# A gated mix of a long convolution and a feed-forward block: one two-stage 2048-point transform through DRAM in place of a four-block transform

## The chip, the cores and the metric

The kernel runs on one core of a Trainium2 chip. Its five engines each work through their own list of instructions: TensorE (PE in the profile, with its weight loads listed apart as PEld), VectorE (DVE), ScalarE (ACT), GpSimd (POOL) and SyncE (SP, which here only issues DMA transfers; SPq in a chain of waits is time spent issuing); 16 DMA engines move data between DRAM and on-chip memory. The time is device microseconds of one execution, median over several executions. A profile covers one execution and shows its span, which is 1.7 to 1.9 us less than the time of the same execution. "PE granted clock" is the share of full TensorE speed that the throttle allowed in a stretch.

## The reference, cut to what matters

There are 2048 tokens and 640 channels. Two things are computed from the same input and mixed with a gate:

```python
x = A_u                                                 # [1, 2048, 640] bf16
g = sigmoid((x * gate_w).sum(-1, keepdims=True))
# a: state-space convolution. For each channel d a kernel K[d, 0..2047] is built from 128 modes:
#    K[d, l] = Re sum_n C[d,n] * dt*B[d,n] * exp(dt*A[d,n] * l)
#    y = irfft(rfft(u, 4096) * rfft(K, 4096))[:2048] + u * Dskip
# b: feed-forward block, 640 -> 1728 -> 640
b = (gelu(x @ w_gate) * (x @ w_up)) @ w_down
return g * a + (1 - g) * b
```

The table K is the sum over 128 modes of complex exponentials. Both kernels split the position l into a coarse part and a fine part, so that exp(a·l) is a product of two short tables ("grid 1" and "grid 2", each with a cosine and a sine half), and the sum over modes is a contraction on TensorE, one small matrix product per channel.

## The kernel before

A helper class collects steps (engine, estimated time, buffers read and written) and orders them per engine with a list scheduler, so the program text isn't the order of execution. The convolution is done in four blocks of 512 tokens, each with a small transform. A product of spectra must therefore be formed for every pair of blocks, which is much work for VectorE:

```python
# parameters and tokens come in the layout of the model and are transposed by the DMA
def x_load(tq, kt):
    dma(1050, lambda: nc.sync.dma_start_transpose(out=xT[tq][:, kt, :], in_=u2[S*tq:S*tq+S, kt*128:kt*128+128]), ...)

# the contraction: one product of 128 weight columns x 84 per channel group and cos/sin half
for g in range(5):
    for q in range(2):
        nc.tensor.matmul(ps[:, k, 84*g:84*g+84], lhsT=cs1[c][:, q, k0+g, :], rhs=cs2[c][:, q, k0+g, :],
                         start=(q == 0), stop=(q == 1))

# spectral products, for block c from all blocks up to c (L904 is the one line tm that all use)
def tm(out, a, b, op):
    nc.vector.tensor_tensor(out=out, in0=a, in1=b, op=op)                     # L904
def mul(x, o, q):  ve(..., lambda: tm(x, u[:, ::1-2*q, rev, ds], kb[:, :, 0:n, ds], ALU.mult), ...)
def comb(x, o, q): ...                     # re*re - im*im and the like, also tm
def fold(x, o): ...
def last(x, o, q): ...
# ... cut: feed-forward gate (L588), up (L606), down (L994), spectra (L846, L866), inverse (L1015)
```

## Time and profile before

| | before |
|---|---|
| time, median of 3 runs | 351.43 us (350.82 to 351.55) |
| span of the profiled run | 355.9 us |
| PE / DVE / ACT busy | 299.7 / 297.8 / 237.2 us |
| moved by DMA | 25.5 MB |

The first fence is from the page of the kernel before: busy time of each engine with its share of the span, then three rows of the picture in 40 equal slices (each digit a busy share in tenths, PEclk the granted clock in tenths of full speed), the load of the DMA queue and the chain of work that ended last.

```profile
PE 299.7 (84%) x2182; PEld 175.8 (49%) x2182; DVE 297.8 (84%) x528; ACT 237.2 (67%) x374; POOL 15.7 (4%) x32
PE   0048459999999999999785679999999999999885
DVE  8999899756368898999893806999999999998962
PEclk9999988999999999999998989999999999999999
...
q1 hardware_dynamic: 52608, 23.79, 26.4%
...
DVE 38%; PE 27%; ACT 19%; SPq 10%; issue 4%; DMA 1%; another core or an unknown queue 0%; DVEq 0%; ACTq 0%
```

Two engines are at 84%, which reads as "nearly balanced", but the rows show that the limits lie in different stages: PE does next to nothing in the first two slices, and DVE is full from slice 26 on. The clock is full almost everywhere. The DMA is at 26%.

The second fence is from the groups of instructions of the kernel before (line, engine, operation, output and inputs, count, busy time and mean of one in ns, then the engine's idle time before them and what ended it).

```profile
L904 DVE TENSOR_TENSOR arena<-arena 128x640 bf16<-128x640 bf16 (+5 forms) x112 | 106.7, 1011 | 1.5 <-ACT arena L998 0.9
L588 PE MATMUL ps<-arena 128*128 128x512 bf16 x280 | 68.5, 396 | 25.9 <-DMA arena<-in_B_w_gate_dram 21.8
L994 PE MATMUL ps<-arena 128*128 128x320 bf16 x448 | 62.0, 299 | 0.4 <-ACT arena L872 0.4
```

The spectral products (L904) cost DVE 106.7 us. Of a matmul, the mean of one (396 ns) runs from its start to its modelled end, and neighbours overlap; busy time divided by count is what it costs: 68.5 / 280 = 0.245 us for 512 columns, and 62.0 / 448 = 0.138 us for 320.

The third is from the table of busy time by stretch of the kernel before (start:end, length, busy time of PE, PEld, DVE, ACT and POOL with instruction count, granted clock, DMA share, GB/s).

```profile
0.00:40.00 40.00, 12.71 (x35) 4.27 (x36) 37.79 (x107) 35.61 (x55) 6.10 (x22) 1.00 0.63 128
...
270.00:310.00 40.00, 40.00 (x315) 29.15 (x314) 39.93 (x42) 6.35 (x8) 0.00 (x0) 1.00 0.17 34
```

At the start PE is busy 12.71 of 40 us; near the end DVE is busy 39.93 of 40 us, and PE is full beside it.

### The profile page before, as it was taken

Reading aid. Unit: us, or ns where it says so; the run is one execution under the profiler, and the core shown is the slowest. Engines: PE = TensorE matmul, PEld = TensorE weight load, DVE = VectorE, ACT = ScalarE, POOL = GpSimd, SP = SyncE. Lnnn points to the kernel's source line nnn. Section 1 sums busy time; section 2 is a strip of 40 time slices with the busy share of each in tenths; the row PEclk is TensorE's granted clock in tenths of the full one; section 3 lists DMA queues with packets and bytes.
Section 4 is the critical chain, followed back from the end, with each engine's and each line's share of the span. In section 5 each row is a group of like instructions: output and inputs, shape, how many; then the busy total and the mean of one; then the engine's idle time right before and its main releaser. Section 6 shows DMA issues by size and latency. Waiting matters only on the chain.

```text
span 355.9 us, 5682 instructions
## 1 busy us (share of the span) xinstructions
PE 299.7 (84%) x2182; PEld 175.8 (49%) x2182; DVE 297.8 (84%) x528; ACT 237.2 (67%) x374; POOL 15.7 (4%) x32
## 2 busy tenths in 40 slices
PE   0048459999999999999785679999999999999885
PEld 0012113444555554444343545666777777767664
DVE  8999899756368898999893806999999999998962
ACT  6999699999999899999964779999111011100000
POOL 6000000000000000000071000000000000000000
PEclk9999988999999999999998989999999999999999
DMA  6684632003100201102552710052400005003321
GB/s 111 181 134 98 163 127 88 20 19 76 37 20 19 58 20 37 40 0 55 187 195 61 276 57 0 2 146 61 103 17 0 20 21 91 20 18 49 100 75 57
DMA packets 53019, 25.46 MB, mean 72 GB/s; under 512 B 46400, under 2 KB 50304, under 8 KB 52608
## 3 DMA queue, kind: packets, MB, share of 16 engines
q1 hardware_dynamic: 52608, 23.79, 26.4%
q0 software_dynamic: 384, 1.31, 1.2%
q8 instruction: 17, 0.28, 0.3%
q14 instruction: 10, 0.08, 0.1%
HBM read 12.83 MB, written 6.03 MB: 53 GB/s over the span
## 4 chain that ended last, share of the span: by engine, by line
DVE 38%; PE 27%; ACT 19%; SPq 10%; issue 4%; DMA 1%; another core or an unknown queue 0%; DVEq 0%; ACTq 0%
DVE arena L904 28%; PE ps L588 10%; PE ps L606 8%; SPq L302 7%; ACT arena L466 5%; ACT arena L529 3%; PE ps L524 3%; DVE arena L883 3%; ACT arena L592 3%; PE ps L1015 2%; ACT arena L430 2%; SPq L307 2%; DVE arena L1024 2%; PE ps L846 2%; ACT arena L660 2%
## 5 line engine op out<-in xcount | busy, mean ns | idle before, releaser
L904 DVE TENSOR_TENSOR arena<-arena 128x640 bf16<-128x640 bf16 (+5 forms) x112 | 106.7, 1011 | 1.5 <-ACT arena L998 0.9
L588 PE MATMUL ps<-arena 128*128 128x512 bf16 x280 | 68.5, 396 | 25.9 <-DMA arena<-in_B_w_gate_dram 21.8
L606 PE MATMUL ps<-arena 128*128 128x512 bf16 x260 | 62.3, 382 | 3.2 <-DVE arena L610 3.0
L994 PE MATMUL ps<-arena 128*128 128x320 bf16 x448 | 62.0, 299 | 0.4 <-ACT arena L872 0.4
L588 PEld LDWEIGHTS <-arena 128*128 128x128 bf16 x280 | 27.9, 101 | 61.7 <-DMA arena<-in_B_w_gate_dram 22.2
L998 ACT ACTIVATE arena<-ps,omg 128x640 bf16<-128x640 f32 x16 | 12.7, 794 | 68.3 <-PE ps L994 61.1
L994 PEld LDWEIGHTS <-arena 128*128 128x128 bf16 x448 | 43.6, 98 | 17.2 <-issue 0.6
L610 DVE TENSOR_TENSOR arena<-ps,arena 128x512 bf16<-128x512 f32 x52 | 34.8, 686 | 17.5 <-PE ps L606 13.7
L466 ACT ACTIVATE arena<-arena 128x2240 bf16<-128x2240 int16 (+1 forms) x20 | 43.3, 2184 | 0.9 <-DVE arena L459 0.8
L606 PEld LDWEIGHTS <-arena 128*128 128x128 bf16 x260 | 24.8, 99 | 33.4 <-issue 7.2
L1015 PE MATMUL ps<-arena 128*128 128x320 bf16 x256 | 37.7, 299 | 2.6 <-DVE arena L1024 1.6
L1015 PEld LDWEIGHTS <-arena 128*128 128x128 bf16 x256 | 24.7, 98 | 12.7 <-issue 3.7
L592 ACT ACTIVATE arena<-ps 128x512 bf16<-128x512 f32 (+1 forms) x56 | 28.5, 615 | 0.3 <-PE ps L588 0.2
L529 ACT CAST arena<-ps 128x420 bf16<-128x420 f32 x32 | 20.3, 674 | 10.9 <-PE ps L524 6.9
L420 ACT ACTIVATE arena<-arena 128x320 bf16<-128x320 f32 x64 | 23.3, 465 | 0.0
L456 DVE SCALAR_TENSOR_TENSOR arena<-arena 128x160 int32<-128x160 f32 x84 | 20.8, 319 | 2.3 <-ACT arena L466 2.2
L846 PE MATMUL ps<-arena 128*128 128x320 bf16 x128 | 20.8, 315 | 1.9 <-ACT arena L850 1.6
L872 ACT CAST arena<-ps 128x640 bf16<-128x640 f32 (+1 forms) x40 | 21.1, 618 | 1.4 <-PE ps L866 0.9
L883 DVE TENSOR_TENSOR arena<-arena 128x640 bf16<-128x640 bf16 (+1 forms) x30 | 11.1, 419 | 12.9 <-ACT arena L872 12.9
L866 PE MATMUL ps<-arena 128*128 128x320 bf16 x144 | 21.1, 299 | 0.8 <-ACT arena L872 0.6
L850 ACT ACTIVATE arena<-ps 128x640 bf16<-128x640 f32 x32 | 20.1, 813 | 1.6 <-PE ps L846 1.6
L655 PE MATMUL ps<-arena 128*128 128x512 bf16 x42 | 13.6, 450 | 8.6 <-ACT arena L660 8.1
(92 smaller groups left out, 310.6 us busy)
## 6 DMA issues: line engine op xcount, KB each, us to landing
out_dram<-arena SPq DMA_DIRECT2D x16, 160.0 KB, 1.8
dFK<-arena SPq DMA_DIRECT2D x9, 256.0 KB, 2.0
arena<-in_B_w_gate_dram SPq DMA_DIRECT2D x13, 160.0 KB, 2.9
arena<-in_B_w_up_dram SPq DMA_DIRECT2D x13, 160.0 KB, 2.7
arena<-in_B_w_down_dram SPq DMA_DIRECT2D x13, 160.0 KB, 2.3
arena<-in_A_u_dram SPq DMA_DIRECT2D x4, 320.0 KB, 4.0
dTAB<-arena SPq DMA_DIRECT2D x1, 1024.0 KB, 4.5
arena<-dTAB SPq DMA_DIRECT2D x1, 1024.0 KB, 5.1
```

Source lines behind the costliest of these rows:

```text
L302: dma(1050, lambda: nc.sync.dma_start_transpose(out=xT[tq][:, kt, :], in_=u2[S * tq:S * tq + S, kt * 128:kt * 128 + 128]), w=[("xT", tq, k ...
L420: nc.scalar.activation(out=e1[:, :, 4 * r:4 * r + 4], in_=quads(aT[:, ds]), func=ACT.Exp, scale=float(sg * (4 + 8 * i)))
L466: ac(actns(2 * n * w), lambda: nc.scalar.activation(out=dst, in_=ph.bitcast(I16)[:, :, :, 0:8 * n:2], func=ACT.Sin, scale=SIN_SCALE), r=[( ...
L529: ac(actns(420), lambda k=k, s=s: nc.scalar.copy(out=kst[:, :, 5 * s:5 * s + 5], in_=ps[:, k, 0:420].rearrange("p (g e) -> p e g", e=84)), ...
L588: nc.tensor.matmul(ps[:, k, :], lhsT=Wg[f % 2][:, kt, :], rhs=xT[tq][:, kt, :], start=(kt == 0), stop=(kt == NKT - 1))
L592: ac(actns(512), lambda: nc.scalar.activation(out=HT[f][0:p, tq, :], in_=ps[0:p, k, :], func=ACT.Gelu_apprx_tanh), r=[("bank", k)], w=[("H ...
L606: nc.tensor.matmul(ps[:, 4 + k, :], lhsT=Wu[f % 2][:, kt, :], rhs=xT[tq][:, kt, :], start=(kt == 0), stop=(kt == NKT - 1))
L610: ve(tt(512, 1) + 60, lambda: nc.vector.tensor_tensor(out=HT[f][:, tq, :], in0=ps[:, 4 + k, :], in1=HT[f][:, tq, :], op=ALU.mult), r=[("ba ...
L846: nc.tensor.matmul(ps[:, k + h, 0:DH], lhsT=tab[:, j, q, fsl(ft)], rhs=src[:, j, h * DH:(h + 1) * DH], start=(j == 0), stop=(j == 1))
L904: nc.vector.tensor_tensor(out=out, in0=a, in1=b, op=op)
L994: nc.tensor.matmul(ps[:, k + h, 0:DH], lhsT=HT[f][:, c, 128 * j:128 * j + 128], rhs=Wd[f][:, h * DH:(h + 1) * DH], start=(f == 0), stop=(f ...
L1015: nc.tensor.matmul(ps[:, k + h, 0:DH], lhsT=tab[:, ft, q, 128 * j:128 * j + 128], rhs=U[ft][:, q, c, h * DH:(h + 1) * DH], start=(ft == 0 ...
```

## The change

Its intent is to take the spectral products off VectorE. The whole sequence gets one 2048-point transform made of two TensorE stages. Between the stages the data must be transposed, which is done by writing to DRAM and reading back in another order. The steps are now:

1. Stage A of u, from token tiles to `dU` in DRAM; stage A of the table K to `dKA`. The table itself goes through DRAM (`dS`) to get from "channel on 32 rows" to "position on partitions".
2. Stage B reads `dU` and `dKA` back, gives the spectra, multiplies them (16 products in all), and applies the inverse of stage B; the result goes to `dY`.
3. `dY` is read back, the inverse of stage A is applied, and the result is mixed with the feed-forward output.

All this is done for two halves of 320 channels, one after the other, and the feed-forward block for two groups of tokens. Inputs are laid out by the host, so that no transposing DMA is left. Tables are laid out in channel quads, so that ScalarE writes runs of four elements. The scheduler is new too: each step carries a rank, and the ranks were tuned with its own estimates of cost.

The diff has 1877 lines; this is its core, with cuts:

```diff
-X2 = [0, 1, 2, 3, 4, 5, 6, 7, 256, 258, 260, 262, 512, 516, 768, 772, 1024, 1280, 1536, 1792, 2048]
+X2 = [1, 2, 3, 4, 5, 6, 7, 8, 258, 260, 262, 264, 516, 520, 772, 776, 1032, 1288, 1544, 1800]
+NE = len(X2)
...
-        dma(1050, lambda: nc.sync.dma_start_transpose(out=xT[tq][:, kt, :], ...
+        dma(640, lambda: nc.sync.dma_start(out=xT[q][:], in_=u_T[q]), w=[f"xT{q}"], rank=1)
...  # the contraction: 20 weight columns, 32 moving columns, four column tiles side by side
+    def contract(h):
+        for b0, nb in ((0, 2), (2, 2), (4, 1)):
+            def go(k, b0=b0, nb=nb):
+                for b in range(nb):
+                    for i in range(16):
+                        for q in range(2):
+                            for cg in range(4):
+                                c = 16 * (b0 + b) + i
+                                nc.tensor.matmul(ps[32*cg:32*cg+NE, k+b, 32*i:32*i+32], lhsT=cs2[:, q, c, cg:4*NE:4],
+                                                 rhs=cs1[:, q, c, cg:128:4], start=(q == 0), stop=(q == 1))      # L678
+            p = pe(128 * nb * 16, go, ...)
...  # the table to DRAM and back
+                    nc.sync.dma_start(out=dst, in_=src)          # L707: 20 writes of 160-byte rows per half
+            dma((m1 - m0) * 3, lambda ph=ph, src=src: nc.sync.dma_start(out=ph, in_=src), ...   # L821: 15 gathers
...  # U with its two halves of partitions exchanged, as the complex product needs it
+                dma(320, lambda c=c, s=s: nc.sync.dma_start(out=Us[c][64*s:64*s+64], in_=U[c][64-64*s:128-64*s]), ...  # L861
...  # the products, 16 in all
+            ve(v2(2560), lambda c=c, t=t: nc.vector.tensor_tensor(out=U[c][:], in0=U[c][:], in1=t[:], op=ALU.mult), ...
+            ve(v2(2560), lambda c=c, t=t: nc.vector.tensor_tensor(out=Us[c][:], in0=Us[c][:], in1=t[:], op=ALU.mult), ...
-        def tm(out, a, b, op):
-            nc.vector.tensor_tensor(out=out, in0=a, in1=b, op=op)
```

Other lines named below: L530 and L550 are the feed-forward gate and up projections, L578 the down projection, L836 stage A of the table, L851 stage B, L880 its inverse, L898 the inverse of stage A, L289 and L293 the evictions from PSUM on ACT and DVE.

## The prediction

> **What bounds the kernel now.** The page gives PE 299.7 us busy (84%), DVE 297.8, ACT 237.2 of a 355.9 us span. The table of engine time by stretch shows stages with different limits. From 0 to 40 us PE is busy 12.7 us: the chain of waits runs through the SP queue, which issues transposing DMAs at 1.26 us apiece. From 230 to 342 us DVE is full (39.7 of 40 us, twice): the chain goes through the spectral products (L904, 106.7 us in all, 28% of the span), and PE stays full beside it only with the down projection (L994, 62 us).
>
> **What the change does.** One two-stage 2048-point transform with DRAM round trips replaces the four-block convolution. Host-laid-out inputs remove the DMA transposes. Costed with durations from the trace, from the groups by shape:
>
> - DVE: products shrink to 16 multiplies of 2560 (1.49 us each): 24 us, for 107 + 11 us of combines. Sine-table phases and multiplies stay near 75 us. New: about 57 PSUM evictions of 640 (about 0.8 us): 46 us; 32 mixes of 320 (0.5): 15 us. Sum about 245 us, 53 less.
> - ACT: 28 gelus of 1024 (1.04 from 0.62 for 512), 18 sines of 2560 (2.34), 104 exponentials (0.364 each), 23 table loads (1.28), about 105 evictions (0.65): about 223 us, 14 less.
> - PE: 540 matmuls of 512 columns (0.216 warm) and about 900 of 320 (0.137) are 240 us. The contraction is now 1280 small ones. [...] L540's 16 matmuls of 100 to 120 columns on 32-column tiles took 0.56 us. Estimate 22 to 25 ns each, 30 us. Sum about 275 us warm; the old program, so counted, is 287.
> - DMA: from 25 to about 55 MB. Packets of 1280 bytes took 62 ns, of 5120 about 220 to 265, so 640 bytes about 35: some 170 us on 16 engines, no bound.
>
> **Stage by stage.** PE starts about 20 us sooner but fills its PSUM pairs until the first gelu, near 29 us. The first contraction waits for DVE (92 us of work before it) and ACT (86): about 107 us. PE has then 195 us left and is the limit: 81 us to the second contraction, which ends near 210. Then the table goes through DRAM: 24 issues of scattered rows and 15 gathers at about 0.5 us, plus 2 us landings, while PE holds 22 us of filler: a stall near 10 us. Then 78 us of PE work (DVE about 72) and a tail of about 10 to 15 us (last spectrum to DRAM, back, 16 mixes, out). Sum about 328 us of span, 324 of time.
>
> **Right or wrong by.** DVE busy near 245 and ACT near 223 on the page; L904-like products 24 us; contraction 13 to 16 us per half; the first contraction near 107 and the second near 195 in the timeline; PE, not DVE, on the last third of the chain; a PE gap of about 10 us before the second kernel half's first stage.
>
> **What would spoil it.** 160-byte writes to DRAM: [...] the trace has only 128-byte loads (13 ns), no such writes[...]. Lock-step between ACT's sines and DVE's phases over two buffers; in-order queues held by one late DMA; small matmuls slower than 25 ns; a cold TensorE clock in the stuttering first third.
>
> Time 324 us, 8 in 10 within 306 to 348. Faster by over 2%: 0.81; within 2%: 0.12; slower: 0.07.

The "22 to 25 ns" of the small matmuls are the estimate; beside it is L540, at 0.56 us for 16, or 35 ns each. "Warm" means a granted clock of 1.0: in the trace of the kernel before, matmuls of 512 columns then follow one another at 0.216 us and those of 320 at 0.136; at a granted clock of 0.5 it is 0.427 and 0.267.

## The result, and the profile after

| | before | after |
|---|---|---|
| time, median of 4 runs | 351.49 us (350.82 to 351.59) | 345.43 us (344.51 to 347.65) |
| span of the profiled run | 355.9 us | 344.3 us |
| PE / DVE / ACT busy | 299.7 / 297.8 / 237.2 | 273.3 / 238.2 / 220.5 |
| mean granted clock in the profile | .98 | .92 |
| moved by DMA | 25.5 MB | 60.7 MB |

The ratio is 0.984, 95% interval 0.980 to 0.987: the change gains 1.6%, where 7.8% was forecast (324 against 351.43). Ratios in this document are the mean time of one kernel's fast runs over that of the other's in the same rounds, so they are not quite the ratios of the medians quoted beside them.

The experiments ran on four chips. On two of them the kernel before took 351.3 and 351.4 us, as above, and on two others 357.4 and 358.0 us. The changed kernel, run again unaltered on one of the latter, took 343.57 us and gave a ratio of 0.964. So the kernel before differs by 1.8% between these runs, and the changed one hardly does; which part of the kernel before that is, no profile here tells. A run more than 1.5% above the fastest of its kernel counts as slow, and fast runs are compared with fast. Medians after "Measured" are over all four runs, but differences are taken between medians of the fast ones: 345.4 us for the changed kernel where the kernel before took 351 us, and 342.6 us (without one slow run of 347.32) where it took 357 to 358 us. Ratios are always to the kernel before.

The same rows of the page as before, now of the changed kernel:

```profile
PE 273.3 (79%) x2785; PEld 155.4 (45%) x2798; DVE 238.2 (69%) x331; ACT 220.5 (64%) x302; POOL 4.0 (1%) x15
PE   0289999988994699999995267439699999899953
DVE  5969887999894258698973044524649865799364
PEclk9999999999998589999998569858989999999995
...
q1 hardware_dynamic: 57958, 60.23, 61.1%
...
PE 49%; DMA 25%; SPq 9%; issue 8%; DVE 4%; ACT 2%; DVEq 0%; ACTq 0%
```

All engines have less work, as forecast. But the row of PE has two valleys (slices 13 and 14, and 22 to 27) in which DVE has little to do as well, the clock falls to 5 or 6 tenths there, and DMA, which was 1% of the chain before, is now 25% of it.

From the groups of the changed kernel: the contraction (L678) with its weight loads, and three of the groups that the prediction had priced.

```profile
L678 PE MATMUL ps<-arena 128*20 128x32 bf16 x1280 | 12.7, 198 | 18.6 <-issue 18.6
L678 PEld LDWEIGHTS <-arena 128*20 128x20 bf16 x1280 | 11.3, 99 | 20.3 <-issue 20.3
L578 PE MATMUL ps<-arena 128*128 128x320 bf16 x448 | 65.2, 306 | 0.5 <-ACT arena L289 0.3
L530 PE MATMUL ps<-arena 128*128 128x512 bf16 x274 | 65.0, 388 | 16.9 <-DMA arena<-in_w_gu_dram 16.0
L289 ACT CAST arena<-ps 128x640 bf16<-128x640 f32 (+2 forms) x110 | 69.4, 692 | 65.8 <-DVE arena L293 26.1
```

The 1280 small matmuls cost PE only 12.7 us, which is 9.9 ns each, but PE stood idle for 18.6 us in between, and "issue" says that nothing which the profile shows was waited for.

The timeline of PE in the second contraction shows the form of that idle time (start, duration, engine and line, count, and in brackets the idle time before and what ended it).

```profile
183.08 1.52 PE L678 MATMUL ps<-arena 128*20 128x32 bf16 x161
186.74 1.24 PE L678 MATMUL ps<-arena 128*20 128x32 bf16 x128 [2.14 <-issue]
193.21 1.24 PE L678 MATMUL ps<-arena 128*20 128x32 bf16 x128 [5.23 <-issue]
```

The matmuls come in bursts of 128 within 1.24 us (9.7 ns each), and then PE waits 2 to 5 us. The stretches of the changed kernel, cut at the marks that the prediction named:

```profile
0.00:101.40 101.40, 81.47 (x470) 40.72 (x476) 88.08 (x143) 87.17 (x114) 3.40 (x14) 1.00 0.51 154
101.40:117.70 16.30, 8.32 (x650) 6.42 (x650) 6.93 (x15) 6.75 (x9) 0.00 (x0) 0.72 0.33 95
117.70:183.10 65.40, 64.54 (x350) 34.62 (x353) 50.02 (x60) 59.90 (x84) 0.00 (x0) 0.97 0.40 104
183.10:202.00 18.90, 6.30 (x642) 5.78 (x642) 2.65 (x4) 3.34 (x5) 0.60 (x1) 0.61 0.45 95
202.00:242.30 40.30, 26.71 (x122) 12.85 (x123) 19.52 (x23) 20.13 (x25) 0.00 (x0) 0.80 0.70 170
242.30:344.30 102.00, 85.94 (x564) 55.00 (x563) 71.03 (x88) 43.22 (x67) 0.00 (x0) 0.95 0.90 276
```

Set against the forecast (the last two rows of the forecast are worked out from its text: 22 us of filler and a stall of 10 us after 210 us, and what is then left to 328):

| stretch | forecast | measured |
|---|---|---|
| start to first contraction | 107 | 101.4 |
| first contraction and the work to the second | 88 | 81.7 |
| second contraction | 15 | 18.9 |
| the table's way through DRAM, to the second half's first stage | 32 | 40.3 |
| the rest | 86 | 102.0 |
| span | 328 | 344.3 |

The program was ahead of the forecast by 12 us when the second contraction started. It lost 4 us in it, 8 us on the table's way through DRAM and 16 us in the rest. On the table's way PE was busy 26.7 us, where 22 us of filler had been priced, and idle 13.6 us for a stall of 10. In the rest PE was busy 85.9 us where 78 had been priced, and idle 16.1 us. The DMA engines were busy 90% of that stretch. The chain of waits of the changed kernel names transfers there (start, duration, what):

```profile
275.14 7.86 DMA arena<-dU
282.99 9.39 DMA arena<-dKA
292.39 14.44 DMA arena<-dY
306.88 1.26 PE ps L898 x8
...
324.94 4.75 DMA arena<-dY
329.74 1.27 PE ps L898 x8
331.03 7.00 DMA arena<-dY
```

A read of 640 KB from `dY` is on the chain for 14.4 us in the thick of the stage and for 4.8 and 7.0 us near the end. In the stretch before, the table's way, the chain is another: 23.5 of its 40.4 us are SyncE's own issuing and 11.2 us are transfers. In the last 102.0 us transfers have 52.0 us of the chain and PE 31.6. SyncE's list on the table's way (here from 214 us; start, duration, line, count) shows table writes (L707), exchanges (L861) and gathers (L821) close behind one another:

```profile
214.10 1.56 SPq L861 DMA_DIRECT2D arena<-arena  x2
215.71 4.17 SPq L707 DMA_DIRECT2D dS<-arena  x7
220.05 1.10 SPq L861 DMA_DIRECT2D arena<-arena  x2
221.20 5.36 SPq L707 DMA_DIRECT2D dS<-arena  x6
...
229.20 6.05 SPq L821 DMA_DIRECT2D arena<-dS  x7
```

### The profile page after: what moved, and what is told of

Read it like the earlier page. It is cut to its first block, busy times and chain, and to the rows that moved or that the text cites. A ratio compares the mean times of both kernels' runs of the same rounds, so it can differ in the third digit from the quotient of the medians.

```text
span 344.3 us, 6849 instructions
## 1 busy us (share of the span) xinstructions
PE 273.3 (79%) x2785; PEld 155.4 (45%) x2798; DVE 238.2 (69%) x331; ACT 220.5 (64%) x302; POOL 4.0 (1%) x15
## 4 chain that ended last, share of the span: by engine, by line
PE 49%; DMA 25%; SPq 9%; issue 8%; DVE 4%; ACT 2%; DVEq 0%; ACTq 0%
PE ps L530 16%; PE ps L578 12%; PE ps L550 10%; DMA arena<-dY 8%; PE ps L880 4%; SPq L707 3%; PE ps L678 3%; DMA arena<-dKA 3%; ACT arena L289 2%; DMA arena<-in_params_dram 2%; DMA arena<-in_w_gu_dram 2%; DMA arena<-dU 2%; PE ps L748 2%; DMA arena<-in_u_nat_dram 2%; DMA dKA<-arena 2%
## 5 line engine op out<-in xcount | busy, mean ns | idle before, releaser
L289 ACT CAST arena<-ps 128x640 bf16<-128x640 f32 (+2 forms) x110 | 69.4, 692 | 65.8 <-DVE arena L293 26.1
L530 PE MATMUL ps<-arena 128*128 128x512 bf16 x274 | 65.0, 388 | 16.9 <-DMA arena<-in_w_gu_dram 16.0
L550 PE MATMUL ps<-arena 128*128 128x512 bf16 x253 | 63.1, 397 | 13.8 <-DMA arena<-in_w_gu_dram 10.3
L293 DVE CAST arena<-ps 128x640 bf16<-128x640 f32 (+2 forms) x62 | 48.4, 800 | 36.6 <-PE ps L678 21.7
L578 PE MATMUL ps<-arena 128*128 128x320 bf16 x448 | 65.2, 306 | 0.5 <-ACT arena L289 0.3
L578 PEld LDWEIGHTS <-arena 128*128 128x128 bf16 x448 | 44.6, 100 | 19.6 <-issue 1.3
L530 PEld LDWEIGHTS <-arena 128*128 128x128 bf16 x280 | 27.6, 99 | 50.6 <-DMA arena<-in_w_gu_dram 16.0
L550 PEld LDWEIGHTS <-arena 128*128 128x128 bf16 x260 | 26.2, 101 | 46.9 <-DMA arena<-in_w_gu_dram 11.7
L554 DVE TENSOR_TENSOR arena<-ps,arena 128x1024 bf16<-128x1024 f32 x26 | 31.7, 1219 | 18.6 <-PE ps L550 16.2
L618 ACT ACTIVATE arena<-arena 128x2560 bf16<-128x2560 int16 x18 | 41.6, 2340 | 1.6 <-DVE arena L614 1.5
L534 ACT ACTIVATE arena<-ps 128x1024 bf16<-128x1024 f32 (+1 forms) x28 | 27.1, 1024 | 7.6 <-PE ps L530 7.4
L678 PE MATMUL ps<-arena 128*20 128x32 bf16 x1280 | 12.7, 198 | 18.6 <-issue 18.6
L851 PE MATMUL ps<-arena 128*128 128x320 bf16 x128 | 22.6, 310 | 5.6 <-DMA arena<-dU 3.0
L639 DVE TENSOR_TENSOR arena<-arena 128x2560 bf16<-128x2560 bf16 x16 | 23.0, 1484 | 3.8 <-ACT arena L618 3.8
L678 PEld LDWEIGHTS <-arena 128*20 128x20 bf16 x1280 | 11.3, 99 | 20.3 <-issue 20.3
L851 PEld LDWEIGHTS <-arena 128*128 128x128 bf16 x128 | 12.5, 101 | 14.7 <-DMA arena<-dU 3.8
L880 PE MATMUL ps<-arena 128*128 128x320 bf16 x128 | 18.7, 299 | 0.0
L904 DVE SCALAR_TENSOR_TENSOR arena<-ps,g_f,arena 128x320 bf16<-128x320 f32 x32 | 15.4, 544 | 2.7 <-PE ps L898 2.7
L666 DVE TENSOR_TENSOR arena<-arena 128x2560 bf16<-128x2560 bf16 x10 | 14.9, 1486 | 3.2 <-ACT arena L618 3.1
L612 DVE SCALAR_TENSOR_TENSOR arena<-arena 128x320 int32<-128x320 f32 x40 | 16.9, 483 | 0.0
```

Source lines behind the costliest of these rows:

```text
L289: nc.scalar.copy(out=dst, in_=src(b))
L293: nc.vector.tensor_copy(out=dst, in_=src(b))
L530: nc.tensor.matmul(ps[:, k + j, :], lhsT=Wg[w][:, kt, :], rhs=xT[2 * grp + j][:, kt, :], start=(kt == 0), stop=(kt == NKT - 1))
L534: add({"ACT": an(1024)}, lambda s: nc.scalar.activation(out=HTall[0:p, :, f, :], in_=ps[0:p, plan.bank(g):plan.bank(g) + 2, :], func=ACT.G ...
L550: nc.tensor.matmul(ps[:, k + j, :], lhsT=Wu[w][:, kt, :], rhs=xT[2 * grp + j][:, kt, :], start=(kt == 0), stop=(kt == NKT - 1))
L554: add({"DVE": v1(1024)}, lambda s: nc.vector.tensor_tensor(out=HTall[:, :, f, :], in0=ps[:, plan.bank(u):plan.bank(u) + 2, :], in1=HTall[: ...
```

## The experiments

Three explanations were to be told apart.

- Supply of instructions. 128 matmuls with their weight loads are 256 instructions. The packets on the instruction queue have 16,384 bytes, 64 for each of 256. In the stretch of the second contraction the list of queues of the changed kernel has:

```profile
q8 instruction: 5, 0.08, 2.0%
```

Five packets in 18.9 us are one per 3.8 us (the four that landed from 191.8 to 203.2 us did so 3.7 to 3.8 us apart), and 5 bursts of 128 are the 640 matmuls of one half. The packet records say more: each of the seven waits before small matmuls that "issue" ended, in both contractions, ended 1.3 to 1.6 us after such a packet had landed, and the program has 22 of these packets for 5583 PE instructions, 254 for each.
- Transfers. In the last 142 us some 35 MB are moved (246 GB/s in the table by stretch over that time, 315 and 292 in its stretches from 249 to 307 us), and the transfers follow one another on the chain: three reads of 7.9, 9.4 and 14.4 us stand there without a break from 275.1 to 306.8 us.
- Issue. SyncE issues all transfers in order, at 0.3 to 1.6 us each on the table's way; the 20 table writes and the gathers of a half may simply take that long to issue.

### Half of the contraction

Edit (mathematically wrong, as it drops one of the two halves of the sum; the result was still within the tolerance):

```diff
-                        for q in range(2):
+                        for q in range(1):
...
-                                                 rhs=cs1[:, q, c, cg:128:4], start=(q == 0), stop=(q == 1))
+                                                 rhs=cs1[:, q, c, cg:128:4], start=True, stop=True)
```

> Half of the small matmuls of both contractions are left out (the imaginary parts; the result is wrong on purpose), order otherwise untouched. In the changed kernel the second contraction took from 183.1 to 201.9 us with PE busy 6.4 us, in bursts of exactly 128 matmuls (256 instructions) apart by 2 to 5 us of 'issue', while DVE was busy 2.7 us and ACT 3.4 of 19. Theory 1 (the instruction stream of PE is the limit there, and everything behind waits): the first contraction falls from 16.3 to about 7 us, the second from 18.8 to about 8, and the whole kernel by 10 to 15 us, since the second one lies on the critical path. Rival (the last stage is bound by DMA bandwidth or by its own latencies, and contraction time is hidden by it): less than 4 us off the whole.

Measured: 329.64 us (326.69 to 332.28), ratio 0.935. The slowest of the four counts as slow; the median of the other three is 328.04 us, 17.4 us below the changed kernel and beyond the 10 to 15 us that were expected. From the groups of this run:

```profile
L678 PE MATMUL ps<-arena 128*20 128x32 bf16 x640 | 6.5, 197 | 2.7 <-issue 2.5
```

PE lost only 6.2 us of work (12.7 to 6.5), but also 16.1 us of idle time (18.6 to 2.5). The second contraction ended at 181.3 instead of 201.9 us, and the 145 us after it stayed about as long as before (142.4). So the small matmuls delay everything behind them, and far beyond their own PE time. The program also has 17 instruction packets in place of 22: five of 256 fewer, for 1280 instructions fewer.

### No exchange of partitions by DMA

Edit (wrong result, relative error 0.26): the 16 transfers of L861, which copy U with its partition halves exchanged (5.2 MB), are dropped, and the second product reads U.

```diff
-                dma(320, lambda c=c, s=s: nc.sync.dma_start(out=Us[c][64 * s:64 * s + 64], in_=U[c][64 - 64 * s:128 - 64 * s]),
+                dma(320, lambda: None,
...
-nc.vector.tensor_tensor(out=Us[c][:], in0=Us[c][:], in1=t[:], op=ALU.mult)
+nc.vector.tensor_tensor(out=Us[c][:], in0=U[c][:], in1=t[:], op=ALU.mult)
```

> The 16 DMA copies that swap the halves of U into Us (5.2 MB, all after 200 us) are left out and the second product reads U instead (wrong result on purpose); PE, DVE and ACT keep every instruction in its order. Theory 2 (the last 140 us are bound by DMA bandwidth: the DMA share is 0.92 to 1.05 from 249 to 307 us): 10 to 17 us less in all, 5.2 MB at some 300 GB/s. Rival (PE with its in-order queue and cold clock bounds the last stage): less than 4 us.

Measured: 333.30 us (332.02 to 334.51), ratio 0.946, 12.1 us below the changed kernel, with all the arithmetic left in. The second contraction ended at the same place (202.1 us). The table's way through DRAM took 32.8 us for 40.4, and the rest 97.8 for 102.0.

### More transfers of the same size

Edit: eight copies from DRAM to DRAM of 640 KB (5.2 MB together, each read and written), issued by GpSimd after each write of `dKA`; nothing waits for them.

```diff
+            add({"POOL": 1000}, lambda s, g=g: nc.gpsimd.dma_start(out=dX[h][8 * g:8 * g + 8], in_=dKA[h][8 * g:8 * g + 8]),
+                r=[(f"dKA{h}", g)], w=[(f"dX{h}", g)], rank=R)
```

> Eight more copies of 640 KB from DRAM to DRAM (5.2 MB), issued on the idle POOL queue as soon as each piece of the table's first stage is written (about 230 to 260 us); nothing waits for them. Theory 2 (DMA bandwidth bounds the last stage): 10 to 17 us more. Rival (PE bound): less than 4 us more.

Measured: 359.14 us (354.96 to 362.79), ratio of the fast runs 1.013. Two of the four runs, the profiled one among them, were slow; the two fast ones, 354.96 and 357.57, are 9.5 and 12.1 us above the changed kernel. Copies that nothing reads, issued from another engine, lengthen the program. This tells transfer volume from issue order: SyncE's list was not touched. It isn't the experiment before with its sign turned, though. In the profiled (slow) run the table's way took 45.0 us and the rest 112.0, so most of the cost fell into the last stage, where dropping the exchange had gained little.

### The table's transfers issued from two engines

Edit: every second table write and gather goes out from GpSimd.

```diff
-                    nc.sync.dma_start(out=dst, in_=src)
+                    (nc.gpsimd if cg % 2 else nc.sync).dma_start(out=dst, in_=src)
```

(and in the same way for the gathers)

> Every second one of the 24 scattered writes of the kernel table and of the 15 gathers of each half is issued on the POOL queue in place of SP; order otherwise untouched. Theory 3 (the way from the end of the second contraction at 201.9 us to its first transform stage at 242 us is set by SP, which issues 24 writes, 15 gathers and the rest at 0.6 to 0.75 us apiece in order, and holds the weight load of PE behind them): that way shrinks from 40 to about 30 us and the kernel gets 5 to 10 us faster. Rival (DMA-bound or PE-bound after it): the way shrinks but the total moves less than 3 us.

Measured: 343.31 us (342.00 to 345.51), ratio 0.978, interval 0.972 to 0.984; against the changed kernel 2.1 us less, which is hardly outside the spread. The table's way took 41.1 us, as before. This doesn't clear SyncE's issuing. The last gather was out 33.3 us after the second contraction's end, where it took 38.7 us before. But PE then waited for a feed-forward weight tile until 235.6 us and did 20 matmuls with it in 6.18 us before the second half's first stage at 241.6 us. Halving the table's issues alone gains little because this other wait takes their place.

### The exchange by VectorE

Edit: the same 16 moves, in the same place of the order, done by VectorE. The result is correct.

```diff
-                dma(320, lambda c=c, s=s: nc.sync.dma_start(out=Us[c][64 * s:64 * s + 64], in_=U[c][64 - 64 * s:128 - 64 * s]),
+                dma(320, lambda c=c, s=s: nc.vector.tensor_copy(out=Us[c][64 * s:64 * s + 64], in_=U[c][64 - 64 * s:128 - 64 * s]),
```

> The 16 swap copies of 64 partitions x 2560 are done by DVE in place of the DMA, at the same place of the order; the result stays right. Leaving them out altogether gave 12 us. Theory 2 (their 5.2 MB stand in the DMA queue before transfers that the chain needs): 8 to 12 us less than the changed kernel, with DVE busy 13 us more if a copy takes about 0.8 us. Rival (the gain of leaving them out came from the product no longer waiting for them, whoever does them): less than 4 us less.

Measured: 334.31 us (333.86 to 336.56), ratio 0.937, 8.3 us below the changed kernel where the kernel before is as slow. The copies are a new group on DVE:

```profile
L861 DVE COPY arena<-arena 64x2560 bf16<-64x2560 bf16 x16 | 13.2, 822 | 0.5
```

13.2 us of work were added to an engine, and the program became 8.3 us shorter. In the chain of waits of this run only one transfer is left in the last stage, the read at the very end:

```profile
309.25 7.62 PE ps L578 x56
319.21 7.06 DMA arena<-dY
327.06 2.15 DVE arena L904 x4
```

The table's way through DRAM took 33.9 us, with 4.2 MB moved in it at a DMA share of 0.50, where the changed kernel moved 6.8 MB at 0.70. The rest took 100.6 us, as long as in the unaltered kernel's second profile (100.5), although its DMA share fell from 0.91 to 0.78: with the transfers off the chain, PE (60.3 us of it) and DVE (14.3 us) hold the last stage to the same length.

### Weight loads first

Edit: PE waits 10 us at 219 us for a feed-forward weight tile, whose load SyncE issued only behind the table writes. Here each weight load is put in SyncE's order as soon as its buffer is free.

```diff
+    for s in early:
+        s["t"] = max([plan.done[d] for d in s["deps"]] + [0]) if s["t"] > 30000 else s["t"]
+    plan.order.sort(key=lambda s: (s["t"], s["i"]))
```

> Weight loads of gate and up stand in the SP queue as soon as their buffer is free, ahead of the scattered writes of the kernel table; order otherwise untouched. In the changed kernel PE waited 10.1 us at 219 to 229 us for one such load. If that wait costs its length, 6 to 10 us less in all. If the way of the table through DRAM (contraction's end at 202 us to the stage at 242 us) is the critical path there, the wait only moves: less than 3 us.

Measured: 346.37 us (343.61 to 347.44), ratio 0.970, against 342.6 of the unaltered kernel on the other chip of that kind: no gain. The conspicuous wait of 10 us was filler that came late: without it the table's way still took 43.5 us, and the chain ran there through SyncE's issues (20 us of them nearly without a break before 240 us). This wait and the table's issues were never taken away together, so what the two cost as a pair is not shown.

### The changed kernel again, and filler between the small matmuls

The first is the changed kernel unaltered. The second puts eight matmuls of 512 columns (results unused) in front of each 128 small ones, 80 in all, which is 17 us at the 0.216 us of a granted clock of 1.0.

```diff
                for b in range(nb):
+                    for _ in range(8):
+                        nc.tensor.matmul(ps[:, k + b, :], lhsT=cs1[:, 0, 0, :], rhs=cs1[:, 0, 0:4, :], start=True, stop=True)
                    for i in range(16):
```

> The changed kernel once more, unaltered, so that the runs of this call have it on their own chip. Every theory expects 343 to 349 us.

> Ahead of each of the ten blocks of 128 small matmuls, PE does eight matmuls of 512 columns more, into the bank that the block overwrites (80 in all, 17 us of array time warm, 160 instructions, the result stays right). Theory 1 (PE waits there for its instructions to be fetched, 16 KB or 128 pairs at a time): the fillers run while the next block is fetched, so each contraction stays within 3 us of its 16 to 19 us and the whole within 3 us of the changed kernel, or below it if the clock stays warmer. Rival (the array or the issue of the small matmuls is itself that slow): each contraction grows by 7 to 9 us and the whole by 12 to 17.

Measured: 343.57 us (342.08 to 347.32; one run slow), ratio 0.964, for the unaltered kernel; 348.44 us (347.50 to 350.09), ratio 0.975, with the filler. From the groups of the run with filler:

```profile
L675 PE MATMUL ps<-arena 128*128 128x512 bf16 x70 | 18.9, 401 | 1.1 <-issue 0.9
L680 PE MATMUL ps<-arena 128*20 128x32 bf16 x1280 | 13.7, 198 | 3.9 <-issue 3.4
```

18.9 us of PE work were added (the trace has 70 of the 80 matmuls; some records of matmuls can be missing) and the program grew by 5.8 us, fast runs compared. That lies between the two expectations, 3 us at most and 12 to 17. The idle "issue" time before the small matmuls fell from 14.8 us in the unaltered run to 3.4. The two contractions grew by 2.0 and 4.2 us only, so two thirds of the long matmuls went into time in which PE had had nothing to run. If the array or the data had been the limit of the small matmuls, the filler would have been added in full. That it isn't free may be due to the filler's own 160 instructions, which must be supplied as well; that isn't shown. The clock, 0.965 in place of 0.938, hides a part of the cost.

### The program planned anew

The planner's own prices explain why it placed the contraction and the transfers as it did: 16 ns per small matmul, no limit on instructions, 450 ns for an issue. Here the exchange is done on DVE or ACT, the prices are close to those of the traces (0.56 us for an issue, 2.24 us for a sine of 2560, which took 2.34, 9.7 ns for a small matmul, and 256 PE instructions supplied per 3.7 us), and the ranks were searched anew with them. The first run keeps the contraction in steps of two PSUM banks; in the second the steps are of one bank and other matmuls may come in between.

```diff
-            p = pe(128 * nb * 16, go, ..., rank=0.5, cr=1.0)
+            p = pe(128 * nb * 9.7, go, ..., rank=P["kc"], cr=0.8, ni=256 * nb)
...
+        def fetched(i, t):
+            lack = S[i]["ni"] - min(512.0, tok + max(0, t - tlast) * 256 / 3700)
+            return t if lack <= 0 else t + lack * 3700 / 256
...   # second run only
-        for b0, nb in ((0, 2), (2, 2), (4, 1)):
+        for b0, nb in ((0, 1), (1, 1), (2, 1), (3, 1), (4, 1)):
```

> A version meant to be better: the swap done on DVE or ACT as in the copy experiment, and the same kernel's planner run again with prices read from the trace (0.56 us a DMA issue, 2.34 us a sine, 9.7 ns a small matmul but only 256 instructions fetched per 3.7 us) and with its ranks searched anew; contraction still in steps of two banks. If theories 1 and 2 name the limits rightly, 312 to 325 us; if the planner's picture is wrong, no better than the copy experiment's 334.

> As v0, and the contraction in steps of one bank (128 pairs, one fetch), so that the planner can put long matmuls between them. Theory 1 expects the idle time of PE before the small matmuls, 18.6 us in the changed kernel, to fall below 8, and the whole to 306 to 320 us.

Measured: 337.04 us (335.35 to 338.42), ratio 0.943, and 331.62 us (328.50 to 335.05), ratio 0.924, interval 0.918 to 0.929. The second is correct and the fastest correct version here: 7.6% below the kernel before and, with the median of its three fast runs at 331.44 us, 11 us below the changed kernel on that chip. Both missed their expectation by more than 10 us. Most of the gain is that of the exchange alone (334.3 us): the new plan with two-bank steps lost 2.7 us against it, and the interleaved one gained 2.9 us. Idle time before the small matmuls was 11.5 and 8.3 us, against 14.8 (the second profile slow). Since the ranks were searched separately for the two, the 5.6 us between them are not shown to be the interleaving's alone. Better prices in the planner brought little beyond the exchange taken off the DMA.

### Both causes taken away together

Edit: the half contraction and the exchange by VectorE in one kernel (again mathematically incomplete).

> Half of the small matmuls (first run) and the partition swap on VectorE instead of DMA (fifth run) together; the maths is as incomplete as in the first run, on purpose. Alone they took 16 us (345.4 to 329.6) and 9 us (343.6 to 334.3) off. If the two are separate causes on one path (fetching of the small matmuls before, transfers in the last stage after), the gains add: 318 to 322 us, which is the forecast of 324 and shows that these two terms are the whole of its error. If they share a cause (what halving gained came from the transfers that it let start earlier, or the other way round), the sum falls short: 326 to 330. On the page: the small matmuls' line near 6 us of busy time with under 4 us of issue, the second half's table in place near 176 us, and DMA share below 0.9 in the last 40 us.

Measured: 316.03 us (314.69 to 318.23), ratio 0.900, interval 0.895 to 0.906, with the kernel before at 351.4 us. The page and the contraction's group of this run:

```profile
PE 262.9 (84%) x2145; PEld 148.4 (47%) x2158; DVE 251.1 (80%) x347; ACT 220.2 (70%) x302; POOL 4.0 (1%) x15
...
L678 PE MATMUL ps<-arena 128*20 128x32 bf16 x640 | 6.5, 198 | 3.0 <-issue 2.8
```

The two gains alone are 17.4 and 8.3 us, together 25.7; the run took off 29.4, so the effects add, and 3.7 us more come on top (or none, if the 12.1 us of the dropped exchange is taken). It lies below the 318 to 322 us that were expected. Where each acts is seen by cutting the spans at the same marks:

| run | second contraction ends | then to the second half's first stage | then to the end |
|---|---|---|---|
| changed | 201.9 | 40.4 | 102.0 |
| changed, again | 198.3 | 41.5 | 100.5 |
| half contraction | 181.3 | 41.2 | 103.8 |
| no exchange | 202.1 | 32.8 | 97.8 |
| exchange by VectorE | 198.0 | 33.9 | 100.6 |
| table issued from two engines | 200.5 | 41.1 | 98.6 |
| weights first | 199.7 | 43.5 | 98.6 |
| more transfers (a slow run) | 201.8 | 45.0 | 112.0 |
| both | 180.9 | 34.5 | 97.6 |

The contraction acts before its own end and the exchange in the table's way through DRAM. The last column lies between 97.6 and 103.8 us in all fast runs and follows neither edit. They are two separate causes. The expectation adds that they would be "the whole of its error", but that isn't shown by this run: half a contraction is less than the prediction had priced, and the forecast's miss has other terms, as follows.

## Why the prediction was wrong, point by point

**What held.** The sums of work: DVE 238.2 us for a forecast of 245, ACT 220.5 for 223, PE 273.3 for 275. That of PE is luck: the contraction took 12.7 us of PE for 30, and the other matmuls 15.6 us more than priced. The 16 products took 23.8 us for 24. The evictions cost 0.82 us on DVE and 0.70 on ACT for 640 elements, as assumed. PE starts earlier and DVE is no longer the limit. The first contraction began at 101.4 us for 107 and the second at 183.1 for 195; why the program was ahead there was not tested. A PE gap "of about 10 us" came too (10.1 us before 229.5 us), but by luck as well: PE waited for a weight tile and not for the table.

**The step that failed: what follows the second contraction.** The prediction gave it 22 us of filler, "a stall near 10 us", "78 us of PE work" and a tail, 118 us in all, with PE as the limit and "no bound" from DMA. It took 142.4 us. Of these PE was busy 112.7, where 100 had been priced, and idle 29.7, where 18 were left for idling. The sign that was named, "PE, not DVE, on the last third of the chain", did not come: transfers have 63.2 us of this chain, PE 34.3 and SyncE's issuing 23.5.

The waits have two parts. On the table's way the prediction counted 39 issues "at about 0.5 us". SyncE issued without much of a break from 202.8 to 240.6 us: 20 table writes in 15.7 us, 15 gathers in 10.3 and, standing among the writes, eight exchanges in 5.6, which the count had left out. That is 0.73 us each. Without the exchange the stretch takes 32.8 or 33.9 us, near the forecast of 32, in place of 40.4 and 41.5. SyncE's time alone is enough to explain that: 5.6 us for the exchanges, and the 20 writes took 12.7 to 13.2 us with none among them, 2.5 to 3.0 less. But the load on the DMA engines falls in the same runs (share 0.50 and 0.57 for 0.70). What stays open is which of the two it is; the same exchange issued from an idle engine's queue, which wasn't run, would tell.

In the rest the volume counts. The prediction divided "some 170 us on 16 engines" by the whole span. It was 60.2 MB and about 210 us, 61% of the span, but 0.90 of the last 102 us, where the reads and writes of `dU`, `dKA` and `dY` are on the chain. 5.2 MB more made the program 9.5 to 12.1 us longer (fast runs), so the stage had no room for more transfers. But fewer of them hardly shorten this stage: without the exchange it took 97.6 to 100.6 us, of which PE was busy 83.7 to 86.2 and idle another 13 to 14, and PE led the chain (53 to 60 us of it). So the part of these 16 us that no run took away is mainly PE's work, under-priced as follows, and its waits for single steps; that is read from the profiles and not tested.

**The mis-sized term: matmuls priced at full clock.** The forecast took 0.216 us and 0.137 us for the long matmuls, the pace that the traces have at a granted clock of 1.0: 245 us without the contraction. The page has 273.3 - 12.7 = 260.6 us. In the trace's clock records the granted clock is either 1.0 or 0.5, and it was 0.61 on average in the second contraction and 0.80 in the 40 us after it. It fell at 108.6 and 187.1 us, where PE had paused 2.3 us at most, between bursts of small matmuls; what made it fall isn't shown. But the clock is the smaller part. In the run with both causes gone, at a mean clock of 0.977, these matmuls still took 262.9 - 6.5 = 256.4 us. The prediction itself says that the kernel before, "so counted, is 287", where its page says 299.7: the price list was known to be 4.4% too low. The same factor on 245 gives 256, within 1 us of that run. Worked out so, the forecast would have been up to 11 us higher. In the last stretch PE was busy 85.9 us where 78 had been priced.

**Right in the sum and wrong in kind: the contraction.** "22 to 25 ns each, 30 us." Busy and idle time together are 12.7 + 18.6 = 31.3 us, so this term didn't cause the miss. But what was priced as PE work is a wait for instructions. A matmul takes 9.7 ns, 128 of them run in 1.24 us, and then the next 256 instructions must come. It goes with the number of instructions here: halving the count took 16.1 us of idle time and 17.4 us of the whole off. The shape of the tiles was not varied. That the limit lies in supply and not in the array or the data is shown by the filler, of which about two thirds ran in the gaps. That the supply is the fetching of instructions rests on the equality of burst and packet size (256 instructions, 16,384 bytes), on the waits that end 1.3 to 1.6 us after a packet lands, and on the five packets fewer at half the count; the speed of fetching itself was not varied. The trace on which the prediction leant spoke for cheap small matmuls more strongly than it said: of L540's eight groups of 16 matmuls on 32 weight columns in the kernel before, seven took 0.39 to 0.40 us, and only one, in a stretch at half clock, the quoted 0.56.

**The fears.** The 160-byte writes were feared; the kernel before has none. In the packet records of the changed kernel the 5120 packets of the table writes took 18.7 ns each on average, against 13 ns for the 128-byte loads of the kernel before: 16% more per byte. On the cold clock, the trace of the kernel before shows this much: the granted clock is 0.5 from 190.0 to 193.4 us, and PE had paused from 187.0 to 190.6. The low clock came, but in the contractions (0.72 and 0.61 on average) and the table's way (0.80). In the first third the table by stretch has 1.00; the clock records begin only at 19.9 us, and the ten matmuls of 512 columns before that followed one another at 0.40 to 0.43 us, the pace at a granted clock of 0.5. The in-order queue did hold a weight load for 10 us, and mending it gained nothing.

**Does it add up?** The miss in the span is 344.3 - 328 = 16.3 us: 12 us ahead at the second contraction, then 4, 8 and 16 us lost. The miss in time is larger, 346.1 - 324 = 22.1 us for the same run. The prediction took 4 us off its span to get a time, from a profile of 355.9 us and a time of 351.4 us of the kernel before, which are of different executions; where both are of one run, the time is 1.8 us *above* the span. That slip is 5.8 us. The under-priced matmuls are 15.6 us of PE busy time, and the exchange alone is worth 8 to 12 us of time. These terms overlap in time, so they are not a sum that must close. A version free of the exchange's transfers and half of the contraction takes 316 us, below the forecast of 324; the correct version that comes closest takes 331.6. A contraction with one matmul for four channels (160 per half instead of 640) would need fewer instructions for the same sums, but would evict more from PSUM; it wasn't built, so what it gives is open.

## What to carry to other kernels

Reckon transfers by stage, not over the span, and their issues with them: 61% on average was 90% in the stage that ended last, and in the stage before it the engine that issues was on the chain for 23.5 of 40.4 us. Moving a copy from the transfers to a VectorE that had room took 8 us off although it added 13 us of engine work. Count instructions as well as columns when matmuls are tiny: here 256 were supplied per 3.8 us (15 ns each) where a burst used them up in 1.24 us (5 ns each), so the supply set the pace, and half as many matmuls were worth 17 us, while long ones put between them lengthened the contraction by a third of their own time. A span and a time are compared only when both are of one execution. And if a price list, applied to the program that was measured, misses its page by 4%, put that factor on the new program too.
